# Stack 0 of a fused attention and long-convolution kernel: rows of keys placed earlier, P·V later, and complex sums in one VectorE operation

## The chip, the cores and the metric

The kernel runs on one core of a Trainium2 chip. The metric is the device time of one execution in microseconds (us). Three runs of the kernel before the change took 999.35, 1000.18 and 1003.87 us; the median is 1000.18. One further execution was profiled, and all rows below are from it.

## The reference

Two independent parts, concatenated along the last axis: multi-query attention with 32 heads (sequence 2048, width 512, head width 16, one key and value head), and an H3-style layer with a short and a long causal convolution, the long one by FFT.

```python
q = (x @ wq).reshape(B, S, H, Dh).transpose(0, 2, 1, 3)
k = x @ wk
v = x @ wv
p = softmax(einsum("bhqd,bkd->bhqk", q, k) * Dh**-0.5)
a = einsum("bhqk,bkd->bhqd", p, v).transpose(0, 2, 1, 3).reshape(B, S, H * Dh) @ wo
...
kv = k_shift * v                      # k_shift: causal convolution of k, 4 taps
y = irfft(rfft(kv, 2 * S) * rfft(ssm_k, 2 * S))[:S]
b = q * (y + kv * ssm_D)
out = concatenate([a, b], axis=-1)
```

## The kernel before

**Stacks and turns.** Attention is cut into 32 *stacks*: four heads by 512 queries. A stack has 16 tiles of 128 keys by 2 pairs of heads, so 32 score tiles of 128 x 1024 (fewer in the last few stacks, where VectorE, called DVE, computes some exponentials itself). One *turn* is one score tile: TensorE (PE) computes the scores of tile t = x + 2 (`scores`, L1055), ScalarE (ACT) their exponential into a tile `p` (`exp`, L1072), and then PE may do the P·V product (L1096) of two older tiles and some *fill*. The table made in `plan` (L1111) says in which turn each P·V stands. I number turns by their score tile, and name what stands behind it on PE up to the next score tile as that turn's. PSUM holds two pairs of banks for scores (`ps`) and two for everything else (`pf`): one for the P·V sums of the running stack, one for fill.

**Fill.** All other work is written as generators ("threads"): the rest of the query, key and value projections (`rest_of_q`, L889), the convolution on PE and on DVE (`conv_pe`, `conv_short`, `conv_dve`), the output projection (`wo_heads`, `wo_part`), and DMAs that spill the transposed x (`spill`). Each yields what it wants next, either a number of PE products, a charge of DVE time, or a wait. `_Fill.turn` (L1412) gives it out at the end of each turn: PE products as far as the planned lateness allows (`LATE`), DVE work as long as a credit of 850 ns per turn is above zero. `em.dve` is the planned time up to which DVE is busy, and `em.ready` holds, for the pairs of banks not in use, the planned times at which DVE will have read them. A fill that needs a new pair waits until `due(ready[0])`. All of this happens when the program is built; on the chip each engine just runs its queue in order, and waits by semaphores.

**Keys and values in stack 0.** The prologue makes only the first two chunks of 256 keys. `rest_of_q` makes the others inside stack 0. It sums x·[wk wv] in one bank (`kv`, L654), copies the sums to SBUF (L907), and then for each chunk places the 16 rows of keys at their partitions by a small product with a mask (`k_chunk`, L674); DVE clips this (`kc`, L680), casts it to f16 (`kh`, L687) and subtracts (`kst`, L689). The tile `kst0` to `kst7` that results holds 256 keys; chunk j is first read by the scores of turn 4j. The values are transposed by `v_turn` (L696) and scaled into `vx` (L699). The last 512 keys (partitions 96 to 128 of the sums, `r` in the code) get the low part of x only later (`x_lo`, L626), and so their own copies (L934).

**The rest of the change's places.** `dft4` (L171) is a butterfly of four complex rows; `both` (L180) does the real and the imaginary part in two DVE operations of 128 x 1024. `product` (L435) multiplies two spectra. `paced` (L141) ties a DMA to an exponential two tiles back. `stack(n + 1)` (L1003) loads the queries of the next stack from DRAM, where `q_send` (L731) and `bound` (L736) put them. Tiles `p` come from a pool of 7; the first four exponentials go into one large buffer, `pfirst`.

Of the kernel before, what the change touches and what calls it, by code (L numbers as in the profile page):

```python
# [69 lines left out]
OWN = NKT - 1  # L70
OWN_IN = (27, 28, 29, 30)
# [38 lines left out]
class _Emit:  # L110
# [30 lines left out]
    def paced(self, dma):  # L141

        u = max(self.pt, default=0)
        if u > 2:
            self.order(dma, self.exps[(u - 2) % 4])
# [13 lines left out]
    def due(self, t):  # L159
        return SLOT * self.now + 300 >= t  # L160

# [9 lines left out]
    def dft4(self, x, e):  # L171
# [8 lines left out]
        def both(out, a, b, op):  # L180
            for part in (re, im):
                yield 0, n
                v.tensor_tensor(part(out), part(a), part(b), op)  # L183
# [251 lines left out]
    def product(self, cx, ch):  # L435
        for i in range(4):
            r = slice(4 * i, 4 * i + 4)
            t = self.w.tile([P, 2, 4, CB], F32, tag="sp", bufs=1, name=self.nm("t"))
            t = t[:, 0], t[:, 1]
            for out, a, b, op in (  # L440
                (t[0], cx[:, 0, r], ch[:, 0, r], ALU.mult),
                (t[1], cx[:, 1, r], ch[:, 1, r], ALU.mult),
                (ch[:, 1, r], cx[:, 0, r], ch[:, 1, r], ALU.mult),
                (ch[:, 0, r], cx[:, 1, r], ch[:, 0, r], ALU.mult),
                (cx[:, 0, r], t[0], t[1], ALU.subtract),
                (cx[:, 1, r], ch[:, 1, r], ch[:, 0, r], ALU.add),
            ):
                yield 0, 1220
# [83 lines left out]
    def conv_dve(self):  # L532
        nat = [0, 1, 2, 3]
        for blk, order in enumerate((("cx", "ch"), ("ch", "cx"))):
# [7 lines left out]
            for i, x in enumerate(self.dft16(cx, f2, f1, 1)):  # L542
                if i == 28:
                    self.seen.add(("soon", blk))
                yield x
# [4 lines left out]
    def load(self):  # L550
# [14 lines left out]
        wqf = [w.tile([P, 2, 4, P], F32, tag="p", bufs=PB, name=self.nm("wqf")) for g in range(2)]  # L565
        wqf = [wqf[g // 2][:, g % 2] for g in range(4)]
# [83 lines left out]
    def kv(self, b, n, cs):  # L650

        i, j = ((0, 0), (1, 0), (0, 1))[n // 4]
        for c in cs:
# [4 lines left out]
                start=n == 0,  # L658
                stop=n == 11,
# [8 lines left out]
    def k_row(self, kmr, b):  # L668
        self.nc.vector.tensor_reduce(kmr, b, AX.X, ALU.max)

# [81 lines left out]
    def prologue(self):  # L752
# [10 lines left out]
        self.exps = [None] * 4  # L763
# [125 lines left out]
    def rest_of_q(self):  # L889
        nc, v, r = self.nc, self.nc.vector, slice(96, 128)  # L890
        n = wg = 0
        while n < 12:
            g = yield 12 - n, 700, CONT if n else NEW, 1
            if n == 0:
                kvb = self.pair()
            for m in range(n, n + g):
                self.kv(kvb[:, 0, :], m, range(4 - (m > 7)))
            n += g
            if n < 12:
                wg += 1  # L900
                v.scalar_tensor_tensor(
                    self.wq[wg][:, 1], self.wqf[wg], WS / LN2, self.wq[wg][:, 0], ALU.mult, ALU.subtract
                )
        assert wg == 3
# [11 lines left out]
        for dp in range(2):  # L916
            yield 0, 1300
            self.x_lo(3, dp, self.xa[:, 2 * dp : 2 * dp + 2])
        self.seen.add("lo3")
        yield 1, 700, CONT, 1  # L920
        self.kv(kvb[:, 0, :], 8, (3,))
        yield 1, 1500, CONT, 1
        self.k_chunk(2, kvb[:, 1, :], 0)
        yield WAIT, 0.5, CONT
        n = 9
        while n < 12:
            g = yield 12 - n, 700, CONT, 1
            for m in range(n, n + g):
                self.kv(kvb[:, 0, :], m, (3,))
            n += g  # L930
        yield 1, 1500, CONT, 1
        self.k_chunk(2, kvb[:, 1, :], 1)
        for h in range(2):
            v.tensor_copy(self.kvt[h][r], kvb[r, 0, CB * h : CB * h + CB])  # L934
        yield WAIT, 1, CONT
        yield 2, 1400, CONT, 2
        self.bound((0,), 0, kvb[:, 0, :])
        self.bound_max((0,), 0, kvb[:, 0, :])
        self.qs.add((0, 0))
        yield WAIT, 0.5, CONT  # L940
        yield 1, 1500, CONT, 1
        self.k_chunk(3, kvb[:, 1, :], 0)
        yield WAIT, 0.5, CONT
        yield 1, 300, CONT, 1
        self.v_turn(r, kvb[:, 0, :])
# [661 lines left out]
```

## Time and profile before

| | |
|---|---|
| median of three runs | 1000.18 us |
| profiled execution | 1002.79 us |
| its span, first to last instruction | 1001.0 us |
| mean granted TensorE clock | 0.991 |
| first exponential starts | 24.39 us |
| last exponential ends | 987.9 us |
| PE / ACT / DVE busy | 942.8 / 953.2 / 750.0 us |

In a row of the timeline stand the start, the length, the engine, the line, the operation, the tile written and the tiles read, the shape, the count, and in brackets how long the engine was idle before it and what ended that. Groups of the page give busy time, the mean of one in ns, and the idle time before. Matmuls overlap, so two that follow each other start closer than their length. `PEld` is the loading of weights, which lies beside PE's products.

### The profile page before, as it was taken

To read this page: it belongs to the slowest core of one execution; us is meant where nothing else is said; L and a number is where in the kernel's file an instruction comes from. 1 tells how busy PE (TensorE), PEld (TensorE's weight loads), DVE (VectorE), ACT (ScalarE), POOL (GpSimd) and SP (SyncE) were. 2 spreads that over 40 slices of the span, in tenths; PEclk is the share of its full clock that TensorE was granted. 3 is DMA by queue.
4 is the path that set the end of the run, shared out by engine and by line. 5 is a ranking of instruction groups with operands and counts; after the bars stand their busy time and mean duration, and the time that the engine had idled before them with its cause. 6 is when DMAs were issued, how large, how long until landed. Compare 5 with 4: busy or idle time off the path is not lost.

```text
span 1001.0 us, 51398 instructions
## 1 busy us (share of the span) xinstructions
PE 942.8 (94%) x23517; PEld 459.5 (46%) x23517; DVE 750.0 (75%) x988; ACT 953.2 (95%) x1032; POOL 172.7 (17%) x321
## 2 busy tenths in 40 slices
PE   8889999989999999999999999999989999998996
PEld 5334445435444444444444455544434444444453
DVE  4555578789539888999898578789989947677743
ACT  5769999999999999999999999999999999999995
POOL 6131122321112000101343332000000122201000
PEclk9979999999999999999999999999999999999999
DMA  7342343332114112321344332111121242221101
GB/s 248 101 115 71 97 137 107 89 101 59 54 51 132 59 41 75 107 66 54 101 131 127 107 111 90 42 54 34 58 85 55 64 128 85 76 65 32 52 7 47
DMA packets 69206, 82.94 MB, mean 83 GB/s; under 512 B 20752, under 2 KB 58294, under 8 KB 68982
## 3 DMA queue, kind: packets, MB, share of 16 engines
q1 hardware_dynamic: 47558, 43.48, 13.8%
q0 software_dynamic: 20320, 35.46, 11.9%
q8 instruction: 186, 3.05, 1.3%
q10 hardware_dynamic: 1104, 0.64, 0.2%
q14 instruction: 38, 0.31, 0.1%
HBM read 54.46 MB, written 25.03 MB: 79 GB/s over the span
## 4 chain that ended last, share of the span: by engine, by line
PE 56%; ACT 27%; DVE 11%; issue 5%; ACTq 0%; DVEq 0%
ACT p L1072 26%; PE f L1096 26%; PE s L1055 16%; PE f L264 11%; DVE sp L183 2%; DVE own L1153 1%; DVE own L1154 1%; DVE ao L1105 1%; DVE sp L304 1%; DVE ao L1106 1%; DVE own L1167 0%; DVE sp L449 0%; DVE t L449 0%; PE f L610 0%; DVE wp L1281 0%
## 5 line engine op out<-in xcount | busy, mean ns | idle before, releaser
L1072 ACT ACTIVATE p<-s 128x1024 f32<-128x1024 f32 x1012 | 935.5, 1069 | 23.5 <-PE s L1055 21.7
L1096 PE MATMUL f<-p,vx 64*32 64x512 f32 (+1 forms) x8848 | 547.5, 556 | 3.4 <-DVE wp L1281 1.1
L1055 PE MATMUL s<-st,kst 49*32 49x512 f16 x8128 | 422.9, 382 | 34.1 <-ACT p L1072 24.3
L1055 PEld LDWEIGHTS <-kst 49*32 49x32 f16 x8192 | 196.6, 90 | 407.7 <-issue 349.5
L1096 PEld LDWEIGHTS f<-p,vx 64*32 64x32 f32 x8848 | 173.6, 106 | 30.9 <-issue 3.9
L183 DVE TENSOR_TENSOR sp<-sp 128x1024 f32<-128x1024 f32 x96 | 111.2, 1214 | 0.0
L304 DVE COPY sp<-f 128x1024 f32<-128x1024 f32 x32 | 39.2, 1224 | 59.2 <-PE f L264 59.2
L309 POOL DMA_DIRECT2D ff<-in_ff x64 | 34.5, 546 | 258.0 <-ACT p L1072 257.1
L264 PE MATMUL f<-wo,o 64*32 64x512 f16 x1440 | 56.8, 375 | 0.4 <-DVE wp L1281 0.2
L183 DVE TENSOR_TENSOR sp<-sp,sp 128x1024 f32<-128x1024 f32 x48 | 56.4, 1217 | 0.3
L1105 DVE COPY ao<-f 128x512 f32<-128x512 f32 (+1 forms) x33 | 22.2, 674 | 43.9 <-PE f L1096 43.9
L264 PE MATMUL f<-xT,wq 64*32 64x512 f16 x1344 | 51.7, 375 | 0.5 <-DVE gm L750 0.5
L309 POOL DMA_DIRECT2D fi<-in_fi x32 | 17.3, 546 | 181.9 <-ACT p L1072 180.0
L264 PE MATMUL f<-a,ff 64*32 64x256 f32 x1024 | 41.6, 378 | 0.7 <-PE s L1055 0.6
L264 PE MATMUL f<-hT,ff 64*32 64x256 f32 x1024 | 40.7, 377 | 1.5 <-DVE sp L304 1.3
L264 PE MATMUL f<-sp,fi 64*32 64x256 f32 x1024 | 40.1, 376 | 0.3 <-DVE r L482 0.3
L484 POOL DMA_DIRECT2D out<-r x32 | 17.2, 543 | 121.8 <-DVE r L482 121.8
L482 DVE TENSOR_TENSOR r<-f,q 128x512 f32<-128x512 f32 x16 | 11.0, 690 | 32.6 <-PE f L264 32.6
L419 DVE TENSOR_TENSOR a<-a,t 128x512 f32<-128x512 f32 x48 | 33.2, 691 | 1.5
L410 DVE TENSOR_TENSOR t<-kk,tpb 128x512 f32<-128x512 f32 (+1 forms) x50 | 33.0, 664 | 0.0
L337 POOL DMA_DIRECT2D hin<-in_B_ssm_k x32 | 20.9, 659 | 58.3 <-ACT p L1072 56.8
L1167 DVE SCALAR_TENSOR_TENSOR own<-own,own 128x1024 f32<-128x1024 f32 x24 | 29.4, 1224 | 0.7
(193 smaller groups left out, 741.4 us busy)
## 6 DMA issues: line engine op xcount, KB each, us to landing
ff<-in_ff POOLq DMA_DIRECT2D x64, 128.0 KB, 2.8
od<-ao SPq DMA_DIRECT2D x60, 128.0 KB
qd<-qp SPq DMA_DIRECT2D x48, 128.0 KB
st<-qd SPq DMA_DIRECT2D x62, 98.0 KB
kk<-in_B_k POOLq DMA_DIRECT2D x32, 128.0 KB, 2.9
v<-in_B_v POOLq DMA_DIRECT2D x32, 128.0 KB, 2.9
hin<-in_B_ssm_k POOLq DMA_DIRECT2D x32, 128.0 KB, 5.7
fi<-in_fi POOLq DMA_DIRECT2D x32, 128.0 KB, 2.8
```

The source lines that it names most:

```text
L183: v.tensor_tensor(part(out), part(a), part(b), op)
L264: y = self.nc.tensor.matmul(out[j : j + 32, cols], w[r, j : j + 32], x[r], start=half == m == 0, stop=half == 1 and m == k - 1,)
L304: self.nc.vector.tensor_copy(out, self.both.rearrange("p i (q n) -> p i q n", q=2))
L309: self.paced(self.nc.gpsimd.dma_start(t[:, i], self.I[n][:, 2 * m2 + i]))
L337: self.paced(nc.gpsimd.dma_start(dst, src))
L410: nc.vector.tensor_tensor(out[:, n], kk[:, x], tap(i, n.stop - n.start), ALU.mult)
L419: nc.vector.tensor_tensor(a, a, t, ALU.add)
L1055: self.nc.tensor.matmul(s[j : j + 32, e, :], self.kst[k // 2][rows, k % 2 * P + j : k % 2 * P + j + 32], self.st[n][rows, a, cols], start= ...
L1072: self.exps[u % 4] = self.nc.scalar.activation(self.pt[u], s, AF.Exp, scale=LN2 * DH**-0.5 / SC / SC)
L1096: nc.tensor.matmul(self.acc[e][32 * j : 32 * j + 32, m], vx[rows, :], y, start=k == 0, stop=stop)
L1105: nc.vector.tensor_copy(a, self.acc[0][:, m])
L1167: v.scalar_tensor_tensor(g, g if i < 4 else y, c[i], y if i else x.bitcast(BF16), ALU.add, ALU.mult)
```

## The change

1. `rest_of_q` is rewritten. The value and key sums go to one pair of banks that is given back at once; the placing products go to a second pair, each in a turn of its own, at points where (by the plan) DVE has read what is overwritten (`read`). The low part of x for keys 1536 on is made in two separate steps, and the last products are added to the copies by an addition (L945 of the new file). The low halves of the query weights are made after the keys, and the last check of the keys (`k_max`) at the very end.
2. The weights `wqf` go from the pool `p` into the pool `ft`, and `pfirst` holds eight tiles. `plan` puts the P·V of stack 0 later.
3. `_Emit.room`: in the first three turns of a stack a fill takes a new pair only if the other pair will be read, by the plan, in time for the stack's first P·V.
4. `both` does both parts in one operation of 2048 elements in the first 24 turns of a stack, and `product` its first two products.
5. Smaller ones: `CROWDED` allows 90 ns more lateness in turns 0 to 63 and 288 to 351; `paced` ties DMAs to the last exponential written instead of the last tile handed out; stack 2 is loaded three turns later; the mark "soon" goes by time left.

```diff
+CROWDED = (0, 64), (288, 352)
...
+    def room(self):
+        s = self.slot % (2 * NKT)
+        return self.due(self.ready[0]) and (s > 2 or self.due(self.ready[-1] - SLOT * (3 - s)))
...
         def both(out, a, b, op):
+            if self.slot % (2 * NKT) < 24:
+                yield 0, 2.3e3
+                v.tensor_tensor(out, a, b, op)
+                return
             for part in (re, im):
...
+    def read(self, less):
+        t = self.dve - less
+        while not self.due(t):
+            yield WAIT, 0.5, CONT
...
         for h in range(2):
-            v.tensor_copy(self.kvt[h][0:96], kvb[0:96, 0, CB * h : CB * h + CB])
-        yield 3, 1500, CONT, 3
-        self.k_chunk(1, kvb[:, 1, :], 0)
-        yield 3, 400, CONT, 3
-        self.v_turn(slice(0, 96), self.bank())
+            v.tensor_copy(self.kvt[h], kvb[:, 0, CB * h : CB * h + CB])
         self.ready.append(self.dve)
         yield WAIT, 0.5, CONT
-        yield 3, 1500, CONT, 3
-        self.k_chunk(1, kvb[:, 1, :], 1)
+        yield 2, 1300, CONT, 2
+        b = self.pair()
+        sums, rows = b[:, 0, :], b[:, 1, :]
+        self.k_chunk(1, rows, 0)
+        yield from self.read(700)
+        yield 3, 400, CONT, 3
+        self.v_turn(slice(0, 96), sums)
+        yield from self.read(0)
+        yield 2, 1300, CONT, 2
+        self.k_chunk(1, rows, 1)
...
-            self.pt.update((i, x[:, i]) for i in range(4))
-        if u > 3:
+            self.pt.update((i, x[:, i]) for i in range(8))
+        if u > 7:
...
-        first = {0: (7,), 4: (8,), 2: (9, 11), 24: (25, 27), 28: (29,)}
-        first.update({x: (x + 4 if x < 26 else 28,) for x in (*range(6, 24, 2), 26)})
+        at = {0: (8,), 8: (11,), 2: (12, 13), 4: (21, 23), 6: (25, 27), 26: (29, 30), 28: (30, 31)}
+        at.update((x, (x + 4,)) for x in range(10, 26, 2))
...
-            if t - self.base[n] == (6 if n > 1 else 22) and n + 1 < NQ:
+            if t - self.base[n] == (6 if n > 1 else 22 + 3 * n) and n + 1 < NQ:
...
-                    if self.holder is None and (i < self.free or not self.em.due(self.em.ready[0])):
+                    if self.holder is None and (i < self.free or not self.em.room()):
```

**PE in stack 0, where chunk 4 is placed.** Before, in turn 15: weights and product of the key sums, the placing product (weights `kv`, moving `msk`), then the next score tile.

```order
L654 LDWEIGHTS wkv_106
L654 MATMUL f_32_386<-xT_122,wkv_106 32x512
L674 MATMUL f_32_386<-kv_475,msk_81 128x256
L1055 LDWEIGHTS kst4_116
L1055 MATMUL s_70_685<-st_22_305,kst4_116 32x512
```

Now, in turn 11:

```order
L662 LDWEIGHTS wkv_108
L662 MATMUL f_41_488<-xT_124,wkv_108 32x512
L687 MATMUL f_41_488<-kv_473,msk_81 128x256
L1074 LDWEIGHTS kst3_117
L1074 MATMUL s_58_583<-st_24_307,kst3_117 32x512
```

Before, the score behind the placing product reads `kst4`, which is made from this very product; now it reads `kst3`, and `kst4` is first read in turn 16. The placings stand, before, in turns 6, 8, 15, 19, 23 and 25 (chunks 2 to 7), now in turns 6, 9, 11, 14, 19 and 23; the transposes of the values in turns 7 and 25, now 8 and 27. Of the P·V products 15 full ones stand in turns 8 to 31 before, and 13.5 now, with 1.5 more in turns 32 and 33.

**DVE in the same place.** Before, from the copies of the sums to chunk 3:

```order
L901 SCALAR_TENSOR_TENSOR wq_6_92<-wqf_2_88,wq_6_92 128x512
L907 COPY kv_475<-f_32_386 96x256
L907 COPY kv_476<-f_32_386 96x256
L680 TENSOR_SCALAR kc_42_492<-f_32_386,msk_81 128x256
L687 CAST kh_43_494<-kc_42_492 128x256
L689 SCALAR_TENSOR_TENSOR kst2_114<-kh_43_494,msk_81,kc_42_492 128x256
L699 TENSOR_SCALAR vx_120<-f_46_509 128x4x3x16
L680 TENSOR_SCALAR kc_49_528<-f_32_386,msk_81 128x256
L687 CAST kh_50_530<-kc_49_528 128x256
L689 SCALAR_TENSOR_TENSOR kst3_115<-kh_50_530,msk_81,kc_49_528 128x256
L626 SCALAR_TENSOR_TENSOR xT_122<-xa_83,xT_122 128x1024 x2
```

Now, the same rows and what follows:

```order
L634 SCALAR_TENSOR_TENSOR xT_124<-xa_83,xT_124 128x1024
L916 COPY kv_473<-f_34_388 128x256
L916 COPY kv_474<-f_34_388 128x256
L693 TENSOR_SCALAR kc_42_490<-f_41_488,msk_81 128x256
L700 CAST kh_43_492<-kc_42_490 128x256
L702 SCALAR_TENSOR_TENSOR kst2_116<-kh_43_492,msk_81,kc_42_490 128x256
L712 TENSOR_SCALAR vx_122<-f_41_488 128x4x3x16
L693 TENSOR_SCALAR kc_49_536<-f_41_488,msk_81 128x256
L700 CAST kh_50_538<-kc_49_536 128x256
L702 SCALAR_TENSOR_TENSOR kst3_117<-kh_50_538,msk_81,kc_49_536 128x256
L693 TENSOR_SCALAR kc_56_577<-f_41_488,msk_81 128x256
L700 CAST kh_57_579<-kc_56_577 128x256
```

Three operations on the query weights ahead of the copies have moved behind the keys, and one of the two on the low part of x has come in their place; chunk 4 follows chunk 3 at once.

**DVE at the start of stack 7.** `f` are pairs of banks, `ao` the copies of the stack just ended, L304 (now L313) the copy of a convolution fill out of its pair. Before:

```order
L1105 COPY ao_639_5249<-f_566_4652 128x512
L1106 TENSOR_TENSOR ao_639_5249<-ao_639_5249,f_566_4652 128x512
L183 TENSOR_TENSOR sp_108_958<-sp_455_3709,sp_108_958 128x4x256
L304 COPY sp_531_4455<-f_628_5141 128x2x2x256
L358 STREAM_TRANSPOSE hT_643_5278<-hin_454_3706 128x256 x2
```

Now:

```order
L313 COPY sp_526_4442<-f_622_5121 128x2x2x256
L1125 COPY ao_639_5273<-f_568_4684 128x512
L1126 TENSOR_TENSOR ao_639_5273<-ao_639_5273,f_568_4684 128x512
L367 STREAM_TRANSPOSE hT_636_5253<-hin_448_3692 128x256 x2
L192 TENSOR_TENSOR sp_118_1082<-sp_449_3695,sp_118_1082 128x4x256 x2
```

The fill's copy has moved from behind the copies of the ended stack to ahead of them: that fill now ends in turn 224 and not in 226, and the next one starts in turn 227 and not in 228. On DVE 1217 operations stand in the program, 1280 before. Of the 63 that are gone 55 are halves of butterflies, 8 of products.

More of the change, by code (lines that the diff above doesn't have):

```diff
@@ L935, in rest_of_q @@
-        yield WAIT, 1, CONT
+        yield 2, 1300, CONT, 2
[8 more added lines that the diff above has]
+        self.k_chunk(1, rows, 1)
+        yield from self.read(700)
+        yield 3, 2500, CONT, 3
+        for m in (8, 9):
+            self.kv(sums, m, (3,), 8)
@@ L1415, in turn @@
         self.late += SCORES + PV * pvs - SLOT
-        room = (LATE - self.late - max(0, SCORES + PV * more - SLOT)) // UNIT
+        room = (LATE + 90 * any(a <= i < b for a, b in CROWDED) - self.late - max(0, SCORES + PV * more - SLOT)) // UNIT
         more = True
```

123 lines of the change are left out of this document (61 added, 62 removed).

## The prediction

> **What bounds the kernel now.** I read the table of engines first, then ScalarE's timeline, then who waited for whom, then PE's timeline in the stretch that the first views point at.
>
> ```profile
> PE 942.8 (94%) x23517; PEld 459.5 (46%) x23517; DVE 750.0 (75%) x988; ACT 953.2 (95%) x1032; POOL 172.7 (17%) x321
> L1072 ACT ACTIVATE p<-s 128x1024 f32<-128x1024 f32 x1012 | 935.5, 1069 | 23.5 <-PE s L1055 21.7
> 24.39:65.26 40.87, 34.81 (x505) 12.56 (x511) 21.25 (x47) 27.30 (x28) 11.26 (x20) 0.83 0.39 113
> 65.26:988.00 922.74, 882.08 (x22827) 432.60 (x22811) 712.41 (x913) 912.33 (x989) 145.37 (x265) 1.00 0.26 77
> ```
>
> The exponentials on ACT pace the program: 935.5 / 1012 = 0.924 us each when nothing holds them up. The two stretches (length, then busy time of PE, PEld, DVE, ACT, POOL, the granted clock, DMA) say where they are held up. In the second, ACT is busy 912.33 of 922.74 us. In the first, which is turns 0 to 27 of stack 0, it is busy 27.30 of 40.87 us, and TensorE is granted 0.83 of its clock. There the chip waits for neither ACT nor DVE (21.25 us busy), so I looked at who ends the waits. The next rows are, in order: ACT's waits from 24 to 70 us and from 70 to 990 us, and PE's from 24 to 66 us (total, times, longest).
>
> ```profile
> ACT p L1072 <- PE s L1055: 12.4, 12, 1.8
> ACT p L1072 <- PE s L1055: 9.2, 14, 1.2
> PE s L1055 <- DVE kst L689: 5.9, 5, 1.6
> ```
>
> ACT waits for scores, and the scores wait for the rows of keys, kst. One such wait in the timeline (the cast to f16 and the rest, that make kst from kc on DVE, are left out):
>
> ```profile
> 42.65 0.69 PE L674 MATMUL f<-kv,msk 32*128 32x256 f32 x2
> 43.39 0.55 DVE L680 TENSOR_SCALAR kc<-f,msk 128x256 f32<-128x256 f32 x1 [2.91 <-PE f L674]
> ...
> 44.83 0.41 PE L1055 MATMUL s<-st,kst 49*32 49x512 f16 x8 [1.49 <-DVE kst L689]
> 45.38 1.02 ACT L1072 ACTIVATE p<-s 128x1024 f32<-128x1024 f32 x1 [1.76 <-PE s L1055]
> ```
>
> From the placing matmul of a chunk to the first score that reads it pass 44.83 - 42.65 = 2.18 us, in which PE has nothing to do, since the next thing in its queue is that score. A second cost hangs on it. These are windows of 3.41 us (the clock is the third last column):
>
> ```profile
> 30.93:34.34 3.41, 2.24 (x24) 1.18 (x24) 2.04 (x6) 2.38 (x4) 0.00 (x0) 1.00 0.36 118
> 34.34:37.75 3.41, 3.41 (x42) 1.10 (x48) 2.73 (x5) 1.96 (x3) 0.00 (x0) 0.50 0.33 110
> 41.17:44.58 3.41, 2.18 (x35) 0.69 (x19) 1.12 (x3) 2.44 (x3) 0.00 (x0) 1.00 0.43 137
> 44.58:48.00 3.42, 3.17 (x66) 1.04 (x66) 0.20 (x1) 2.57 (x3) 0.22 (x1) 1.00 0.22 72
> 48.00:51.41 3.41, 1.92 (x43) 0.75 (x35) 2.05 (x5) 1.58 (x3) 3.31 (x6) 1.00 0.27 75
> 51.41:54.82 3.41, 3.41 (x49) 0.75 (x41) 1.46 (x4) 2.64 (x3) 1.13 (x2) 0.50 0.31 69
> 54.82:58.23 3.41, 1.82 (x34) 0.61 (x26) 2.74 (x6) 1.29 (x2) 1.07 (x2) 1.00 0.56 105
> 58.23:61.64 3.41, 3.09 (x30) 1.18 (x14) 0.23 (x1) 2.05 (x2) 1.24 (x3) 0.50 0.91 293
> 61.64:65.06 3.42, 3.42 (x50) 1.13 (x56) 2.43 (x8) 1.13 (x2) 1.82 (x4) 0.50 0.35 104
> ```
>
> Of the four windows in which PE was busy 2.24 us or less, three were followed by one or two at half clock. Four windows at half clock are 13.65 us, and cost PE up to half of that, 6.8 us.
>
> **The rows of keys (the main term).** In the order of before, chunks 4, 5 and 6 are placed one turn ahead of their first score, with nothing between. In the changed order every placement from the second on stands three to six turns ahead: PE works through at least two score tiles and a P·V product in the 2.18 us. So PE's waits for kst at 44.83, 50.70 and 57.72 go, and the wait for vx:
>
> ```profile
> 50.70 0.41 PE L1055 MATMUL s<-st,kst 49*32 49x512 f16 x8 [1.49 <-DVE kst L689]
> 57.72 0.41 PE L1055 MATMUL s<-st,kst 49*32 49x512 f16 x8 [1.59 <-DVE kst L689]
> 60.91 1.22 PE L674 MATMUL f<-kv,msk 32*128 32x256 f32 x2 [0.32 <-DVE vx L699]
> 33.62 0.41 PE L1055 MATMUL s<-st,kst 49*32 49x512 f16 x8 [0.67 <-DVE kst L689]
> ```
>
> That is 1.49 + 1.49 + 1.59 + 0.32 = 4.9 us. The wait at 33.62 stays: chunk 2 is placed just as before, straight behind the copies of kv, and the transpose that filled PE meanwhile (0.55 us) moves behind turn 8, so it grows to 1.2 us: +0.5. The final check on the keys (k_max, one small product of 0.3 us) leaves this stretch.
>
> Without low-activity windows PE keeps its clock. One is left, around that 1.2 us wait, and by the rows above I let it cost one window at half clock, 1.7 us; 6.8 - 1.7 = 5.1 us are saved. **Term: 4.9 - 0.5 + 0.3 + 5.1 = 9.8 us, taken as 9.6** because a few scores now are followed by something other than P·V, which costs PE 0.11 us each (below).
>
> Can PE use this, or is ACT or its own work late next? Full-clock prices, from one start to the next:
>
> ```profile
> 39.04 0.41 PE L1055 MATMUL s<-st,kst 49*32 49x512 f16 x8
> 39.26 1.05 PE L1096 MATMUL f<-p,vx 64*32 64x512 f32 x16
> 40.12 0.40 PE L1055 MATMUL s<-st,kst 49*32 49x512 f16 x8
> 71.22 0.83 PE L245 MATMUL f<-xT,wq 128*32 128x512 f16 x12
> 71.98 0.41 PE L1055 MATMUL s<-st,kst 49*32 49x512 f16 x8
> 82.59 0.40 PE L1055 MATMUL s<-st,kst 49*32 49x512 f16 x8
> ```
>
> A score tile is 0.22 us ahead of P·V (39.04 to 39.26) and 0.33 ahead of the rest (its 0.41 less an overlap of 0.07, as at 71.98), a P·V 0.86, twelve query products 0.76, a placement 0.69 at most (42.65). From turn 8 to turn 46 the new order holds 38 scores (8.4, and 1.8 for some 16 dearer ones), 22 P·V (18.9), 48 query products (3.0), five placements (3.4) and seven small products, which I estimate at 0.33 like a score (2.3): 37.8 us. ACT needs 38 × 0.924 = 35.1. So **PE becomes the bound** by 2.7 us, its waits being gone. Turn 8 starts at 33.6 as now, so turn 46 starts near 71.4, or 73.1 with one window at half clock, against 82.59 (the last row): 9.5 us, which agrees with the term. ACT alone would allow 9.5 + 1.7 + 2.7 = 13.9: the upper bound; the lower is nothing, if each wait returns elsewhere. Eight held tiles let 1.5 P·V (1.3 us) slide from stack 0 to turns 32 to 34; the 37.8 us contain them, so they cost nothing more.
>
> The Trainium skill, "TensorE: Matmul & The Clock Gate", section "HAM oscillation", gives "no PE-idle gaps >~3.4µs" as the rule that keeps the clock. The rows differ: no wait here is longer than 1.59 us, and the clock was halved three times. By the page the remaining 1.2 us wait would cost no clock, and the sum would be 1.7 us more.
>
> **Starts of stacks (room).** In before, a fill that ends just ahead of a stack's first P·V leaves its PSUM pair to that P·V:
>
> ```profile
> 253.82 1.09 PE L1096 MATMUL f<-p,vx 64*32 64x512 f32 x16 [1.04 <-DVE sp L304]
> 255.24 88.34 ACT L1072 ACTIVATE p<-s 128x1024 f32<-128x1024 f32 x96 [1.09 <-PE s L1055]
> 344.74 50.75 ACT L1072 ACTIVATE p<-s 128x1024 f32<-128x1024 f32 x55 [1.16 <-PE s L1055]
> 553.78 154.32 ACT L1072 ACTIVATE p<-s 128x1024 f32<-128x1024 f32 x167 [0.56 <-PE s L1055]
> ```
>
> These are stacks 7, 10 and 17. In the new order the readers of those pairs stand one to four turns earlier. Each delay is the wait and the 0.18 us of restarting the overlap (1.10 instead of 0.92 us between two exponentials), so 1.09 + 1.16 + 0.56 + 0.54 = **3.4 us**. What comes next there, the pair of the stack just ended, is read by operations that stand ahead of that copy on DVE. Bounds: 0, and all of the 9.2 us that ACT waits after 70 us.
>
> **Two parts in one operation.** 63 instructions fewer on DVE.
>
> ```profile
> L183 DVE TENSOR_TENSOR sp<-sp 128x1024 f32<-128x1024 f32 x96 | 111.2, 1214 | 0.0
> L419 DVE TENSOR_TENSOR a<-a,t 128x512 f32<-128x512 f32 x48 | 33.2, 691 | 1.5
> ```
>
> No row has 2048 elements. From 691 and 1214 ns, 523 ns for 512 more, I estimate 2.26 us, against 2 × 1.21: 0.17 us less for a pair, some 10 us of DVE in all, less if DVE overlaps the ends of its operations. DVE is idle 25% of the time and waits for PE, so I take **0** on the path. Uncovered it could give what DVE delays PE by, within the 9.2 us; it can cost, too, since whatever stands behind one waits up to 1.05 us longer (2.26 - 1.21) (a rival below). The other edits (later v, tables in another pool, DMAs paced by the tile done, the lateness of 90 ns allowed in two stretches, the later stack load) I take at 0: they are hidden by ACT's 0.37 us of slack per tile (0.924 less 0.55 from a score's start, 44.83, to its exponential's, 45.38). Bounds -1 to +2 us.
>
> **Sum.** 9.6 + 3.4 = 13.0 us off the profiled execution's 1002.79 (span 1001.0) gives 989.8. That execution lies 2.6 us above the median of three, 1000.18; part of this may be its windows at half clock, which the change removes. I take half of it off: **988.5 us**.
>
> **Rivals.** (1) *The clock stays low*: PE is bound in stack 0 with little slack, and if low windows come from something other than these waits (window 41.17 was as idle as 30.93, and no half clock followed), only the waits go: 13.0 - 5.1 = 7.9, so 992 to 995. By the rule of the Trainium skill named above, the waits were too short to halve the clock, which would be this rival; three of four windows speak against it. (2) *The stack's own load becomes late*: the faster stack 0 leaves less time for the queries of stack 1.
>
> ```profile
> 55.48 0.66 SPq L1011 DMA_DIRECT2D st<-qd  x2
> 69.16 0.41 PE L1055 MATMUL s<-st,kst 49*32 49x512 f16 x8
> ```
>
> From the issue of that load to turn 32 there are 13.7 us now, and some 8 then, and a spill DMA now stands just ahead of it on SP. Each us by which it lands later than that is paid one for one; 2 to 4 us give 991 to 993. (3) *Slower*: the 2.26 us operations sit ahead of PSUM reads. If one holds a pair beyond what the schedule allowed, PE waits 1.05 us longer, 0.37 of it covered, so 0.68 us each. From 20 of the 63 on (13.0 / 0.68) the gain is gone; with 35 it would be 988.5 + 23.8 = 1012. Against it: the schedule charges them with 2.3 us and leaves them out of each stack's last quarter. (4) *The order doesn't do what it says*: DVE's queue delays the rows, so that the waits return at turns 12 to 28; only the starts of stacks and 2 to 3 us remain, 996 to 998.
>
> **Chances.** Forecast 0.62 (its own range 985 to 992), (1) 0.15, (2) 0.08, (3) 0.06, (4) 0.05, ACT as the only bound with the clock full (984 and less) 0.04. The range for 8 in 10, 984.5 to 996, holds the forecast, (1) and (2). A measurement of this kernel can tell about 0.5% from no change, so faster means below 995.2: 0.88; same 0.06; slower 0.06.
>
> **What would show it.** Right: turn 46 starts near 72 to 73 us; PE waits for kst only ahead of turns 0 and 8; at most one or two windows at half clock ahead of 66 us; no wait of ACT over 0.5 us at turn 6 of stacks 7, 10 and 17; 2048-element rows near 2.26 us. Wrong: waits of PE for DVE behind 2.2 us operations, ACT waiting at turn 32 for a load, or half clock as often as now.

## The result and the profile after

The changed kernel took 991.29, 991.43, 991.82 and 991.97 us, median 991.62. Four runs of the kernel before, the three above among them, gave a median of 1002.02 us. The ratio is 0.9895, with a 95% interval of 0.9859 to 0.9930. The profiled execution took 991.43 us, its span is 989.7 us, 11.3 us less than the span of before.

These are the rows of the changed kernel that answer to the first ones of before: engines, the group of exponentials, and the same two stretches (the first is turns 0 to 27 of stack 0, again up to the start of the scores of turn 28 on PE; the second ends with the start of the last P·V; length, busy PE, PEld, DVE, ACT, POOL, granted clock, DMA).

```profile
PE 941.1 (95%) x23565; PEld 463.0 (47%) x23565; DVE 747.5 (76%) x925; ACT 951.4 (96%) x1032; POOL 174.0 (18%) x321
L1092 ACT ACTIVATE p<-s 128x1024 f32<-128x1024 f32 x1008 | 929.9, 1069 | 13.9 <-PE s L1074 12.7
24.26:57.84 33.58, 32.24 (x505) 12.22 (x503) 16.64 (x35) 26.95 (x28) 5.67 (x9) 0.85 0.23 74
57.84:976.98 919.14, 883.09 (x22869) 436.48 (x22867) 714.47 (x862) 910.95 (x989) 152.25 (x276) 1.00 0.27 80
```

The first stretch is 7.3 us shorter (40.87 before). PE is now busy in 32.24 of its 33.58 us, and its clock is still only 0.85. The second is 3.6 us shorter (922.74 before). The waits: ACT's from 24 to 66 us and from 66 to 990 us, then PE's for keys from 24 to 66 us, and one of PE's from 66 to 990 us that the kernel before does not have.

```profile
ACT p L1092 <- PE s L1074: 5.7, 7, 1.6
ACT p L1092 <- PE s L1074: 7.0, 6, 4.3
PE s L1074 <- DVE kst L702: 0.7, 1, 0.7
PE f L674 <- DVE ks L673: 4.2, 1, 4.2
```

Of ACT's 14 waits in the later part 6 are left, but one of them is 4.3 us long. Its cause is in the last line: the final check on the keys (`k_max`), which the change moved from stack 0 to the end of the query work. This is its place in the timeline, PE and DVE (the rows that matter are PE's product and the DVE rows ahead of it):

```profile
733.35 0.69 DVE L1260 TENSOR_TENSOR o<-of,r 128x512 f16<-128x512 f32 x1 [3.36 <-DMA r<-rd]
...
734.80 0.69 DVE L1260 TENSOR_TENSOR o<-of,o 128x512 f16<-128x512 f32 x1
735.41 0.67 DVE L757 TENSOR_SCALAR gn<-f 40x512 f16<-40x512 f32 x1
...
736.01 0.67 DVE L763 TENSOR_REDUCE gm<-f 48x1 f32<-48x512 f32 x1
...
736.61 2.27 DVE L306 TENSOR_REDUCE gx<-xT 128x1 f32<-128x2048 f16 x1
...
738.80 0.21 DVE L673 TENSOR_SCALAR ks<-msk,ks 128x4 f32<-128x4 f32 x1
...
739.06 0.59 PE L674 MATMUL f<-ks,msk 128*128 128x4 f32 x2 [4.23 <-DVE ks L673]
```

A DVE operation of 0.21 us, on four elements a partition, stands behind a queue that ends in a reduction of 2.27 us. That queue was late itself: ahead of its first row here DVE had stood idle for 3.36 us, waiting for a transfer. PE's product waits 4.23 us for it, and all scores wait behind the product. Exponential after exponential, ACT is late by 4.46, 1.21 and 0.36 us over its usual 0.924: 6.0 us in all, the last two of them behind work at half clock.

The wait ahead of turn 8 stayed. PE's row names ACT, but the exponentials before it ran without a break; the weights of the same product, the tile kst, say what was late (the weight load is the first row):

```profile
33.16 0.11 PEld L1074 LDWEIGHTS <-kst 49*32 49x32 f16 x8 [1.45 <-DVE kst L702]
33.16 0.41 PE L1074 MATMUL s<-st,kst 49*32 49x512 f16 x8 [1.15 <-ACT pfirst L1092]
```

The last view shows windows of 3.41 us around it: four in stack 0, then the window that holds most of the wait for the check and the two behind it.

```profile
30.65:34.06 3.41, 2.08 (x38) 0.96 (x30) 1.93 (x5) 2.88 (x4) 0.00 (x0) 1.00 0.38 127
34.06:37.48 3.42, 3.42 (x34) 1.09 (x42) 1.68 (x4) 2.62 (x3) 0.00 (x0) 0.50 0.20 68
37.48:40.89 3.41, 3.41 (x34) 0.79 (x26) 0.31 (x1) 1.02 (x1) 0.00 (x0) 0.50 0.00 0
40.89:44.30 3.41, 3.41 (x56) 1.12 (x40) 2.15 (x4) 2.51 (x3) 0.00 (x0) 0.50 0.02 5
...
733.80:737.21 3.41, 1.03 (x24) 0.20 (x8) 3.34 (x6) 2.25 (x3) 0.00 (x0) 1.00 0.23 60
737.21:740.62 3.41, 1.56 (x18) 0.89 (x26) 2.59 (x9) 0.28 (x1) 0.00 (x0) 0.50 0.26 79
740.62:744.03 3.41, 3.41 (x48) 0.99 (x40) 3.38 (x5) 2.30 (x3) 0.00 (x0) 0.50 0.00 0
```

So three things were open: what the moved check costs, whether the wait ahead of turn 8 is what halves the clock in stack 0, and what took ACT's later waits away (the sum over turns 33 and on of what the exponentials' starts lie apart beyond 0.924 us fell from 8.9 us to about zero outside the check).

### The profile page after: what moved, and what is told of

The parts are those of the page before. It is cut to its first block, busy times and chain, and to the rows that moved or that the text cites. A ratio compares the mean times of both kernels' runs of the same rounds, so it can differ in the third digit from the quotient of the medians.

```text
span 989.7 us, 51425 instructions
## 1 busy us (share of the span) xinstructions
PE 941.1 (95%) x23565; PEld 463.0 (47%) x23565; DVE 747.5 (76%) x925; ACT 951.4 (96%) x1032; POOL 174.0 (18%) x321
## 4 chain that ended last, share of the span: by engine, by line
PE 50%; ACT 36%; issue 7%; DVE 6%; DMA 1%; SPq 0%; ACTq 0%; DVEq 0%
ACT p L1092 35%; PE f L1116 23%; PE s L1074 15%; PE f L273 9%; DMA r<-rd 1%; DVE sp L188 1%; ACT xT L630 1%; DVE sp L456 0%; PE f L618 0%; PE f L662 0%; PE f L687 0%; DVE o L1260 0%; PE f L254 0%; DVE ao L1125 0%; ACT pfirst L1092 0%
## 5 line engine op out<-in xcount | busy, mean ns | idle before, releaser
L1074 PEld LDWEIGHTS <-kst 49*32 49x32 f16 x8192 | 199.0, 89 | 401.9 <-issue 352.9
L313 DVE COPY sp<-f 128x1024 f32<-128x1024 f32 x32 | 39.1, 1222 | 62.1 <-PE f L273 62.1
L188 DVE TENSOR_TENSOR sp<-sp 128x2048 f32<-128x2048 f32 x36 | 82.3, 2287 | 0.9
L188 DVE TENSOR_TENSOR sp<-sp,sp 128x2048 f32<-128x2048 f32 x19 | 43.4, 2286 | 0.4
```

The lines of the kernel that those rows point to most:

```text
L188: v.tensor_tensor(out, a, b, op)
L313: self.nc.vector.tensor_copy(out, self.both.rearrange("p i (q n) -> p i q n", q=2))
L1074: self.nc.tensor.matmul(s[j : j + 32, e, :], self.kst[k // 2][rows, k % 2 * P + j : k % 2 * P + j + 32], self.st[n][rows, a, cols], start= ...
```

## The experiments

All times are medians, and the ratio is to runs of the kernel before that were taken beside them on the same chip. Three chips were used, and they ran the kernel before at 1005.8 to 1007.6 us; so ratios are to be compared, or times that stand beside the same time of the kernel before.

| kernel | us | before | ratio, 95% interval |
|---|---|---|---|
| changed, again (after_again) | 991.81 | 1006.37 | 0.9869, 0.9839 to 0.9900 |
| changed, without the rule `room` (no_room) | 991.42 | 1005.83 | 0.9852, 0.9831 to 0.9874 |
| check's DVE part early (kx_early) | 988.75 | 1005.83 | 0.9823, 0.9802 to 0.9843 |
| check in stack 1 (kx_pair) | 986.43 | 1006.37 | 0.9810, 0.9778 to 0.9841 |
| placements as filler (fill) | 992.35 | 1005.83 | 0.9864, 0.9845 to 0.9883 |
| transposes as filler (v_first) | 990.76 | 1005.83 | 0.9847, 0.9823 to 0.9871 |
| full products as filler (fill_full) | 990.56 | 1006.37 | 0.9853, 0.9823 to 0.9884 |
| 63 operations split again (split_ops) | 991.60 | 1006.37 | 0.9868, 0.9838 to 0.9899 |
| before, merged operations alone (merged) | 1006.26 | 1007.56 | 1.0006, 0.9986 to 1.0025 |
| that and a mended list (aligned) | 994.56 | 1005.95 | 0.9896, 0.9860 to 0.9931 |
| changed, surplus in the list (stale) | 997.19 | 1005.95 | 0.9909, 0.9877 to 0.9941 |
| both repairs (best) | 984.04 | 1007.56 | 0.9770, 0.9748 to 0.9792 |

**The changed kernel again**, as the point of reference for the kernels measured beside it:

> The changed kernel itself, for comparison with the other kernels of this call: 991 to 993 us, ratio 0.985 to 0.990.

Measured: 991.81 us, 0.9869. As expected.

### The check on the keys

```diff
         v.tensor_scalar(self.gm[:, 16:17], km, self.cut, None, ALU.mult)
+        kx = self.ks[:, 4:8]
+        v.tensor_scalar(kx, self.msk[:, 291:295], km, LIM, ALU.mult, ALU.min)
...
-        self.k_max(b, km)
+        nc.tensor.matmul(b, self.msk[:, 0:P], kx, start=True, stop=True)
```

> The final check on the keys is changed alone: its small operation on DVE (4 elements a partition, 0.21 us) is issued in stack 0, where its input is made, and only its product stays at the end of the queries. Theory: PE's wait of 4.23 us at 739 us is the place of that operation in DVE's queue, behind a reduction of 2.27 us and four others. The wait goes, the two windows at half clock behind it (737.2 to 744.0) go, and with them ACT's delays of 4.46 + 1.21 + 0.36 = 6.0 us: 991.6 - 6.0 = 985.6. Rival: DVE is late there anyway, and the operations behind the product (the reduction that reads its bank) or the next fill wait in its place: 989 to 991.

Measured: 988.75 us, some 3 us less and not 6. The product still waits, now for another DVE operation (PE's timeline):

```profile
736.30 0.38 PE L1018 MATMUL f<-ks,msk 128*128 128x4 f32 x2 [1.49 <-DVE gm L763]
```

Both theories had a share: the small operation was what ended last, and right behind it stood the reader of the bank that the product writes, `gm` in the rows above. A wait for several things names only the last of them. The next kernel takes both away: the early operation as above, and the product in the spare bank of the pair of stack 0's first query products.

```diff
-                b = self.bank()
+                b = self.pair()
+                b, x = b[:, 0, :], b[:, 1, 0:4]
...
+        nc.tensor.matmul(x, self.msk[:, 0:P], kx, start=True, stop=True)
+        self.k_row(kmr, x)
```

> The whole final check on the keys stands in stack 1: its small operation on DVE is issued where its input is made, and its product goes into the spare bank of the pair that the first query products of stack 0 fill, behind them. Theory: what PE waits for at 739 us is first the small operation (4.23 us) and, once that is early, the reading of the bank that the product takes (1.49 us with the operation early); with both early no wait is left there and no window at half clock between 700 and 980 us. The product costs 0.3 us of PE in stack 1. 6.0 us less than the changed kernel in this call, 5 to 6.5. Rival: DVE is behind its schedule at 736 us by about 4 us whatever stands there, and the next product that needs a bank read by DVE waits instead: 2 to 3 us less only.

Measured: 986.43 us, 5.4 us less than the changed kernel beside it (983.54 to 987.82 against 990.33 to 993.78 in single runs). Between 61 and 970 us PE has one wait for DVE left, ACT waits 3.2 us, and there is one window at half clock, at 214 us behind that wait of PE:

```profile
PE f L273 <- DVE hT L367: 0.7, 1, 0.7
ACT p L1093 <- PE s L1075: 3.2, 4, 1.4
```

So the move of the check cost 5.4 us. The rival fell: nothing else took its place.

### The clock in stack 0

Three kernels put something on PE into the wait ahead of turn 8. The first repeats the placement of the same rows twice:

```diff
         self.k_chunk(1, rows, 0)
+        for _ in range(2):
+            nc.tensor.matmul(sums[:, 0:CB], self.msk[32:64, 163:291], self.kvt[0][32:64, :], start=True, stop=True)
```

> Two further placing products of the same rows (0.69 us each with what lies behind them, results overwritten) stand behind the placement of chunk 2, ahead of turn 7, in the 1.15 us for which PE waits ahead of turn 8. Theory of the clock: the window 30.65 to 34.06, in which PE is busy 2.08 of 3.41 us, is what halves the clock from 34.06 to 44.30. With PE busy throughout, no window at half clock is left ahead of 700 us, turn 46 starts at 72 to 73 us and not at 75.9, and the time is 991.6 - 3 = 988.6. Rival: the clock follows something other than this wait (the kind of products in this stretch): half clock stays, turn 46 stays at 75.9 or comes 0.3 later, 991.5 to 992.5.

Measured: 992.35 us, three windows at half clock, turn 46's exponential at 76.97 us: the rival's numbers. But the trace shows that this tested the theory only in part. The extra products write into the pair that DVE is reading, so they wait themselves, and the window ahead of the half clock has PE busy in 2.73 of 3.41 us:

```profile
31.94 1.13 PE L924 MATMUL f<-kv,msk 32*128 32x256 f32 x4 [0.64 <-DVE kc L693]
```

The second puts the transposes of the values back where they stood before the change:

```diff
         self.k_chunk(1, rows, 0)
-        yield from self.read(700)
-        yield 3, 400, CONT, 3
         self.v_turn(slice(0, 96), sums)
```

> The transposes of the values (0.55 us on PE) stand straight behind the placement of chunk 2 again, as before the change, in the wait ahead of turn 8. Theory of the clock: PE is busy 2.08 + 0.55 = 2.6 us in the window of the wait, above the 2.24 us after which windows at half clock followed so far, so no window at half clock or one is left, turn 46 starts at 72 to 74, and the time is 988.5 to 990. Rival: a wait of 0.6 us is enough, or the wait has nothing to do with it: three windows at half clock as now, 991.6.

Measured: 990.76 us and again three windows at half clock, from 32.53 us on; the transposes waited for the same 0.64 us, and PE was busy 2.58 us in the window ahead. So the 2.24 us that the forecast's rows suggested are no limit. The third uses full products into a bank that DVE has finished with:

```diff
         self.k_chunk(1, rows, 0)
+        for _ in range(5):
+            nc.tensor.matmul(kvb[:, 1, :], self.wq[0][:, 0, 0, :], self.xT[0][:, 0, 0, :], start=True, stop=True)
```

> Five products of 128 rows by 128 columns by 512 elements (f16, results unused, some 0.22 us each) are put behind the placement of chunk 2, into a bank that nothing reads late, in the wait ahead of turn 8. The extra placements and the transposes tried there before waited themselves for DVE, so PE stood still for 0.6 us more. Theory: with the window ahead of 34 us filled (over 3.0 of 3.41 us) the clock stays full, no half clock ahead of 700 us, turn 46 some 3 us earlier than in the changed kernel of this call, 2 to 3.5 us less in all. Rival: the clock is halved for what PE does between 30 and 44 us (placements on 32 rows, sums of keys on 32 columns, few products of values), not for its waits: three windows at half clock as before, 0 to 1 us more.

Measured: 990.56 us, and no window at half clock ahead of 558 us. PE's timeline of this kernel: the filler, turns 7 and 8 with no wait, and turn 46; then the window.

```profile
31.25 1.25 PE L924 MATMUL f<-xT,wq 128*128 128x512 f16 x5
32.43 0.78 PE L1076 MATMUL s<-st,kst 49*32 49x512 f16 x16
...
71.33 0.94 PE L1076 MATMUL s<-st,kst 49*32 49x512 f16 x16
```

```profile
29.60:33.00 3.40, 3.22 (x42) 1.14 (x34) 2.08 (x5) 2.02 (x3) 0.00 (x0) 1.00 0.37 123
```

Turn 46 starts at 71.33 us; in the changed kernel's profile it is 75.86. Against the changed kernel beside it only 1.25 us are gained, less than the 2 to 3.5 expected and less than the runs scatter (989.18 to 992.60 us here, 990.33 to 993.78 there). The traces show two reasons. First, half clock in stack 0 is not the same in every execution. Profiles of kernels whose stack 0 is that of the changed one, or nearly, gave:

| kernel | half clock in stack 0, us | turn 46's exponential, us |
|---|---|---|
| changed (first profile) | 10.24 | 76.39 |
| changed (after_again) | 3.41 | 73.37 |
| changed (no_room, the same program) | 10.24 | 76.71 |
| kx_early | 10.24 | 76.09 |
| split_ops | 6.83 | 74.67 |
| kx_pair | 6.83 | 75.06 |
| stale (below) | 6.83 | 75.61 |
| fill_full | 0 | 71.86 |
| best | 0 | 72.16 |

Between the first two, 6.83 us of half clock cost 3.0 us, of which 0.25 us lie ahead of the first exponential already. Second, PE waits at 558 us for the transfer of a table in fill_full (1.82 us, and a window at half clock behind it), which the slower kernels do not show. From issue to landing these transfers took 3.9 us there (median of six), against 2.5 us in the changed kernel's first profile; why they were slower stays open.

### What took the later waits away

The forecast gave the waits at the starts of stacks to the rule `room`. One line puts the old condition back:

```diff
-                    if self.holder is None and (i < self.free or not self.em.room()):
+                    if self.holder is None and (i < self.free or not self.em.due(self.em.ready[0])):
```

> The changed kernel without the rule that keeps a fill from starting ahead of a stack's first products while a pair is read late. Theory (the forecast's): waits of ACT of 0.5 to 1.3 us come back at turn 6 of some stacks, two to four of them at 1.1 + 0.2 us: 994 to 997. Rival: the other edits have moved the fills of those stacks anyway, and the rule decides nothing: 991 to 992.5.

Measured: 991.42 us. More than that: the two programs are the same, instruction for instruction, on every engine. The rule decides nothing in the changed kernel, and this run is a third measurement of it. The rule asks for a second entry only in a stack's first three turns, and there, wherever the first entry was due in the changed kernel, the second was due too: a fill that waits for the right entry comes late enough by itself.

Next, the merged operations alone in the kernel before (`both`, `product` and the mark "soon" as in the change, nothing else), and the changed order with each merged operation as two:

> The kernel before with one part of the change alone: the butterflies' two parts (and the first two products of a block) in one operation, charged with 2.3 us in the schedule. Theory: the waits at the starts of stacks 7, 10 and 17, which the forecast gave to the rule on a stack's start, go through the moved fills alone, since that rule turned out to change no instruction of the changed kernel; with the waits of PE for the readers of the spectra they are worth 3 to 5 us, so 0.995 to 0.997 of the kernel before. Rival: merged operations do nothing by themselves (within 1 us of the kernel before), and the later waits went because stack 0 ends earlier and shifts all fills.

> The order of the changed kernel, but each of its 63 operations of 2048 elements as two of 1024, one behind the other. The rows of the changed kernel give 2.286 us for one against 2 x 1.215 = 2.43 us: 63 x 0.144 = 9 us more of DVE. Theory (the forecast's): on the path this is worth nothing: within 1 us of the changed kernel. Rival: what stands behind them on DVE is late by up to 0.14 us for each in a row, and PE's wait at 739 us grows by 0.3 to 1 us, so 1 to 3 us more.

Measured: merged 1.0006 (0.9986 to 1.0025), no difference; ACT's waits after turn 33 grew to 11.0 us, and those at turn 6 of a stack now stand in stacks 5, 11 and 14 (before: in 5, 7, 10 and 17). split_ops 991.60 us, 0.2 us from the changed kernel. For merged the first half of the rival holds: by themselves the merged operations take none of the later waits away. For split_ops the theory holds: the 9 us of DVE are worth nothing on the path.

That leaves the list. The old `rest_of_q` keeps one pair from its first product to the check on the keys. Each time its products were followed by a step without the mark `CONT`, by which a thread says that it keeps its pair (the low part of x, the reduction of the keys and the end lacked it), the planner took the pair for given back and put a time into `ready`, the list of planned times at which pairs have been read: three entries for one pair. From then on the list held two more than there were free pairs, and since taking a pair drops the first entry, a fill started once the pair *two allocations back* had been read. In the own block of the last stacks, where the list is read at the same point in both kernels, it holds three times in the kernel before, the first of them 15 to 20 us older by the plan than the right one, and one in the changed kernel. The new `rest_of_q` takes two pairs and gives back two. So I mended the list in the kernel with merged operations, with the old stack 0:

```diff
             if n == 0:
+                del self.ready[:2]
                 b = self.bank()
```

> The kernel before with merged operations, and with one line that drops two entries from the planner's list of the times at which PSUM pairs have been read, once stack 0's own fills are issued. In the kernel before that list holds two entries more than pairs are free, so that a fill is started by the reading time of a pair two allocations back; in the changed kernel, whose rewritten stack 0 takes two pairs where the old one kept one, the surplus is gone. The allowance of 90 ns in the two crowded stretches is taken over too, since without it the stricter rule leaves fills over at the end. Stack 0 stays as before. Theory: the list is what removed ACT's waits after turn 33 (8.9 us in the kernel before, 11.0 with merged operations alone, about 0 in the changed kernel outside the check on the keys): 8 to 11 us less, ratio 0.989 to 0.993, and no row of PE waiting over 0.5 us for a DVE reader of a spectrum or of the own block. Rival: the later waits went because all fills shifted with the shorter stack 0: they stay within 2 us of the 11.0, ratio 0.998 to 1.001.

and spoiled it in the changed kernel:

```diff
             if n == 0:
+                self.ready[:0] = [0, 0]
                 b = self.bank()
```

> The changed kernel with two surplus entries (times long past) put back into that list at the same place, everything else kept. Theory: fills start again before their pair is read, and ACT's waits after turn 33 come back in part or whole, at starts of stacks and in the own block's four stacks: 5 to 9 us more than the changed kernel of the other calls, ratio 0.992 to 0.996. With two surplus entries the rule on a stack's start has something to decide again, and may keep its share (waits at turn 6 of a stack, 3 us in the kernel before) away. Rival: the list has nothing to do with it: ratio 0.985 to 0.989 as for the changed kernel.

Measured: aligned 994.56 us, 0.9896, as the theory expected. stale 997.19 us is 5.4 us above the 991.81 of after_again, as expected, but its ratio, 0.9909, falls short of the expected 0.992, and its interval reaches into the rival's range. What settles it is its trace: by the measure used above, the starts of exponentials from turn 33 on, stale loses 10.0 us outside the check on the keys, where the changed kernel and aligned lose none. The rows are ACT's waits after turn 33, and PE's for the own block, of merged; of aligned, where PE has none for the own block; and of stale, where 3.5 us of ACT's waits are the check on the keys once more.

```profile
ACT p L1076 <- PE s L1059: 11.4, 16, 2.2
PE f L1059 <- DVE own L1158: 3.9, 4, 1.0
```

```profile
ACT p L1078 <- PE s L1061: 2.8, 6, 1.1
```

```profile
ACT p L1093 <- PE s L1075: 12.7, 17, 2.4
PE f L1075 <- DVE own L1176: 3.9, 4, 1.0
```

One place in PE's timeline shows the mechanism. It is the own block's second product of stack 26: in the kernel before and in the changed one.

```profile
831.10 0.41 PE L1055 MATMUL f<-st,kst 49*32 49x512 f16 x8
...
834.11 0.41 PE L1055 MATMUL f<-st,kst 49*32 49x512 f16 x8 [0.99 <-DVE own L1154]
```

```profile
825.16 0.41 PE L1074 MATMUL f<-st,kst 49*32 49x512 f16 x8
...
828.83 0.41 PE L1074 MATMUL f<-st,kst 49*32 49x512 f16 x8
```

Before, the product was put in a turn too early, and PE waited 0.99 us for DVE; with the right entry it stands 3.67 us behind the first one instead of 3.01, past another score, and waits for nothing. aligned also has the allowance of 90 ns of the change. The allowance alone was not tried, but stale has it too, and there the waits are back. In stale P·V products show no wait for a DVE reader of their pair, as they did at three starts of stacks before: with the surplus, `room` does decide one case. Its share was not measured apart.

### Both repairs

> Both repairs together: the check on the keys in stack 1 (5.4 us less than the changed kernel, measured alone) and five products with unused results in the wait ahead of turn 8 (1.3 us less, measured alone, with a wait of 1.8 us for a table's transfer in its profiled run that no other run shows). Theory: they add up, 985 us or less on this chip, ratio 0.977 to 0.980, no half clock ahead of 200 us, turn 46's exponential at 71.5 to 72.5. Rival: the full clock of that one profile was luck of where the windows of 3.41 us lie: half clock again in stack 0, turn 46 at 73 to 77, and 986 to 987 us as with the check alone.

Measured: 984.04 us, ratio 0.9770. That is 2.4 us below kx_pair, which ran on another chip (the intervals of the two ratios just overlap), and by the ratios 1.0% below the changed kernel. No half clock ahead of 200 us in a second profile with the full products, turn 46's exponential at 72.16 us; one window at half clock is left later, at 210.84 us, behind the wait for hT that kx_pair shows too. The two windows around turn 8 are these:

```profile
28.31:31.72 3.41, 3.22 (x45) 1.18 (x38) 1.21 (x4) 3.04 (x4) 0.00 (x0) 1.00 0.28 90
31.72:35.13 3.41, 3.12 (x42) 1.42 (x48) 1.32 (x4) 2.28 (x4) 0.00 (x0) 1.00 0.32 109
```

The theory holds, except that the wait for a table's transfer is back at the same place, 1.04 us, so it was no accident of one run:

```profile
561.24 0.42 PE L273 MATMUL f<-a,ff 64*32 64x256 f32 x4 [1.04 <-DMA ff<-in_ff]
```

## Why the prediction was right, and where it was not

988.5 us was predicted, 991.62 measured, inside the forecast's own range, near its upper end. But the sum was right for partly wrong reasons: two terms were off by about 5 us each, in opposite directions, and that they nearly cancel is luck. The chain of kernels gives the terms in ratios: merged operations 1.0006; with the mended list 0.9896; with the new stack 0 on top, without the moved check's cost, 0.9810 (kx_pair); with that cost 0.9869. In us of a kernel of 1006: 0, 11, 9 and back 6. Each interval is some 0.3% to either side, so each term is good to 4 or 5 us; the traces, below, are closer. The last step of the sum was not borne out either: it took 1.3 us off because the profiled execution lay above the median of three, but with the fourth run that median is 1002.02 us. Without this step the sum is 989.8 us, a gain of 13.0 us where 10.4 were measured.

**The rows of keys (9.6 us predicted).** The mechanism was right, and one size was not. PE's waits for keys are gone except at turns 0 and 8, and PE is what bounds stack 0. Turn 46 starts at 75.86 us in the first profile, against 82.59: 6.7 us. In after_again, with one window at half clock as I had assumed, its exponential starts at 73.37 instead of 83.14 us: 9.8 us, of which 0.4 us lie ahead of the first exponential. Without any half clock (fill_full) turn 46 starts at 71.33, where I had worked out 71.4 from the prices of PE's products. That close a hit is luck in part: turn 8 starts there at 32.81 and not at 33.6, so the way from turn 8 to turn 46 took 38.5 us and not 37.8. What was mis-sized is the number of windows left at half clock: one assumed, and three, one and three in three profiles of the same program. At the forecast's own 1.7 us a window, two more are 3.4 us, about what the first profile lacks. So two of the forecast's signs failed there: turn 46 at 72 to 73 us, and at most two windows at half clock. Rival (1) was thus half true: in two profiles of three the clock stayed low although only the one wait that the forecast had named was left.

By the section on oscillation in the Trainium skill, "TensorE: Matmul & The Clock Gate", which the forecast set against its rows, a wait of 1.15 us should not cost the clock. Here it went with half clock in every profile that had it, and in neither of the two in which full products filled it. The same page's section "What's actually happening" says that the window in which activity is counted runs freely and does not start with the program. This agrees with three profiles of one program: half clock began at 34.06, 35.37 and 34.55 us, and lasted 10.24, 3.41 and 10.24 us.

**Starts of stacks (3.4 us predicted).** The waits at turn 6 of stacks 7, 10 and 17 are gone, and so is one that the forecast left out of its sum, 1.04 us at turn 6 of stack 5 (195.22 us in the kernel before). In ACT's timeline after turn 33 the first breaks are now in stacks 6 and 9:

```profile
62.19 153.51 ACT L1092 ACTIVATE p<-s 128x1024 f32<-128x1024 f32 x165
216.45 89.46 ACT L1092 ACTIVATE p<-s 128x1024 f32<-128x1024 f32 x97 [0.74 <-PE s L1074]
306.15 429.90 ACT L1092 ACTIVATE p<-s 128x1024 f32<-128x1024 f32 x467 [0.24 <-PE s L1074]
```

But the step failed: `room` did not do it. The list's surplus went, and with it nearly all later waits: 8.9 us instead of 3.4. The forecast took the names of the planner's quantities at their word. The bound that I gave, all of ACT's 9.2 us, was where the value lay.

**Two parts in one operation (0 predicted).** Right for the time. The rows are 2.286 us where 2.26 was estimated, so a pair saves 0.14 us, and neither putting them in (merged) nor taking them out (split_ops) changes the time. Rival (3), that they delay PE's readers, did not come about in the changed kernel: none of its waits of PE over 0.15 us stands behind such an operation. But the delay exists. In merged, with the surplus in the list, a stack's first P·V waits 2.18 us for a reader that stands right behind one. The first row is of the changed kernel, the others of merged:

```profile
L188 DVE TENSOR_TENSOR sp<-sp 128x2048 f32<-128x2048 f32 x36 | 82.3, 2287 | 0.9
...
372.32 2.29 DVE L451 TENSOR_TENSOR t<-sp,sp 128x2048 f32<-128x2048 f32 x1
374.52 1.28 DVE L720 TENSOR_SCALAR cut<-f 128x512 f32<-128x512 f32 x2
375.86 1.09 PE L1100 MATMUL f<-p,vx 64*32 64x512 f32 x16 [2.18 <-DVE cut L720]
```

**The other edits (0, bounds -1 to +2).** Wrong by the check on the keys: 5.4 us. The forecast counted that the check leaves stack 0 (0.3 us gained), and did not ask where it goes. Its DVE operation joined a queue that had just lost 3.36 us to a transfer, its product stood on PE ahead of all scores, and its bank had a reader still to come. This is outside the bounds that I gave, and none of the four rivals was it.

**Rivals (2) and (4).** Stack 1's load did not come late: PE shows no wait for it at turn 32. The order did what it says, apart from `room`.

## What to carry to other kernels

Where a step moves, price its arrival as well as its departure: each instruction of it joins the end of a queue on its engine. Here a DVE operation of 0.21 us made PE wait 4.23 us, because of what stood ahead of it on DVE, and everything behind its product on PE waited too. Where a planner decides the order, read what its accounts hold at the points that matter, not what their names say; here two surplus entries in a list cost some 9 us of ACT's time, and the edit that was written against such waits decided nothing. And a sum that comes out right is no proof of its terms: only kernels with one part each showed that 5 us had been missed on either side.

## What the hardware showed unasked

Half clock can outlast the wait that it follows. In the first profile PE was busy in all of the window 34.06 to 37.48 us and of the next two, and the clock came back only at 44.30; in after_again it came back after one (35.37 to 38.78 us). What PE runs there (placements on 32 rows, sums on 32 columns, few P·V) may count for less than its busy time, or the position of the windows may decide; the runs do not tell. Nor is there one busy share that separates the cases: after 2.73 of 3.41 us (fill) and 2.58 us (v_first) the clock was halved, after 3.12 and 3.22 us (best) it was not, yet the window at 41.17 us of the kernel before, with 2.18 us, was not followed by half clock either. All fourteen profiles together, without the first 20 and the last 16 us of each, hold 3829 windows at full clock with another window behind them. All 11 in which PE was busy for less than 1.8 us were followed by half clock, 22 of the 196 between 1.8 and 2.74 us, and none of the 3622 above, among them windows with sums on 32 columns (27.24 to 30.65 us of the changed kernel, 3.41 us busy). So thin products alone did not cost the clock. The full products both filled the wait and did denser work than what waited there in the other two kernels, and this was not separated.
